# How a fused attention and MLP kernel makes the product of state and W1, and which engine rounds

## The chip, the cores and the metric

The kernel runs on one core of a Trainium2 chip. The metric is the device time of one execution in microseconds (us). The five instruction queues are those of TensorE (PE, matrix products), VectorE (DVE), ScalarE (ACT), GpSimd (POOL) and SyncE (SP, which issues the DMAs). "PEld" is PE's load of a stationary operand.

## What is computed

```python
def _attn_ref(x, state):                       # B, H, S, Ns, D = 8, 8, 512, 32, 64
    scores = scale * x @ state.T
    a = softmax(scores)                        # over the 32 state rows
    xread = a @ state
    a2 = softmax(scale * state @ x.T)          # over the 512 rows of x
    sread = a2 @ x
    return concatenate([xread, sread], axis=2)

h = attn @ w_in                                # 512 -> 1024
solu = h * softmax(h)
y = (layer_norm(solu) * g_ln) @ w_out          # 1024 -> 512
z = y @ w3                                     # 512 -> 2048
out = (z * sigmoid(1.702 * z)) @ w4            # 2048 -> 512
```

There are 8 batches of 512 rows of x and 32 rows of state per head: 4608 token rows in all. The weights arrive as 64-bit floats and are brought to float32 on the chip.

## The kernel before

**Numbers.** Most products are made from split operands: a float32 tile is written as hi + lo, both in the rounded format fp32r, and `mm3` (lines 421 to 424) issues hi x hi, hi x lo and lo x hi into the same PSUM tile. `split` (line 454) makes the pair: first a cast to hi, then lo = w - hi. A few products take plain float32 operands (fp32) and are one matmul in the code; the trace shows two for each.

**The state's product with W1.** Since xread @ W1 is a @ (state @ W1), the kernel makes V = state @ W1 for each batch and then multiplies the 512 rows of a by V. V has four tiles of 128 x 512 per batch: two groups g of four heads, two halves f of W1's 1024 columns. For batches 0 and 1 `state_w1` (line 664) makes a tile with two fp32 matmuls whose stationary operand is 64 columns of the transposed state (`stT`) and whose outputs are the two halves of one PSUM tile's partitions; ACT rounds it out of PSUM to `vhi`, and DVE subtracts for `vlo`. From batch 2 on (`DIRECT = 2`) `state_w1_both` (line 679) makes V of two batches at once, while the even one of the pair is in its turn. The two batches' transposed states are put side by side and split (`sthi`, `stlo`), and every product is a `mm3` of 128 columns with the split W1 (`W1s`). Its PSUM tile holds half a tile of each batch, so four copies for each (g, f) bring the halves into float32 tiles `v`, which then pass through `split` to `hi_v` and `lo_v`. The odd batch is called turned: in its scores, reads and copies the two head pairs of a group change places.

**Which engine.** A step may name several engines with costs. The cast of `split` and that of the attention rows (`ahi`, line 609) may go to ACT or DVE, the subtraction to POOL or DVE.

**Order.** Nothing is issued in the order of the code. Each call of `do` records a step with its tiles; `Plan.plan` puts all steps in an order, by due times worked out backwards from keys that PE's steps carry, by planned costs per engine and by the free tiles of the SBUF slots (71 of kind "s") and of the eight PSUM banks; `emit` then issues each engine's list. Each engine works through its own list in that order and waits at an instruction whose inputs aren't there. In the attention stage PE's list for one batch b holds the transposes of x (until batch 2; later ones are made by DMA and DVE), the scores (`psc`, line 571), the transposes of exp (`e2t`, line 621), the reads of x (line 633), the V steps, and between them the first MLP's products of the batches before (`mlp1`, `z_T` at line 827, `mlp1_out`). Also in this stage W3's blocks are converted (lines 443 to 451), summed (line 880), split and written back to HBM, in groups `w3_00`, `w3_10`, `w3_01` (a fourth comes later). The second MLP follows and keeps PE full.

Of the kernel before, what the change touches and what calls it, by code (L numbers as in the profile page):

```python
# [8 lines left out]
F32 = mybir.dt.float32  # L9
# [16 lines left out]
KF = 11.222  # L26
LOOK = 27.436
KR = 1.553
DIRECT = 2
W1S = 20.477  # L30
ATT = -0.491
ZL = 7.738
M1B = -7.631
VST = 25.191
RK = 6
LEAD = 62.849
KEEP = 5
# [306 lines left out]
def attention_solu_gelu(ctx: ExitStack, tc: tile.TileContext, x, state, w1, w2, g_ln, w3, w4, out):  # L344
# [52 lines left out]
    def PE(c):  # L397
        return [("pe", c)]
# [55 lines left out]
    def split(w, name, due, shape=(512,), pair=None, low=(("pool", 1.23), ("dve", .6))):  # L454

        hi, lo = pair or [tl("s", [P, *shape], F32R, f"{h}_{name}") for h in ("hi", "lo")]
        do([("act", .52), ("dve", .335)], lambda e: copy(e, hi(), w()), [w], [hi])
        do(list(low), lambda e: e.tensor_tensor(lo(), w(), hi(), op=ALU.subtract), [w, hi], [lo], key=due)  # L458
        return hi, lo

# [43 lines left out]
    def attention(b):  # L504
# [5 lines left out]
            n_step[0] += 1  # L510
            return base + (n_step[0] - 1) * SLOT / steps[0]

        both = b >= DIRECT
        turned = both and b % 2
        xt = {}
        load_x(b, 0)
        if not turned:
            load_state(b)
        for j in range(1, NP):
            load_x(b, j)  # L520

# [43 lines left out]
        def scores(g):  # L565
            p = tl("m", [P, 512], F32, f"psc{b}_{g}")

            def go(e):
                for i in range(2):
                    jj = i ^ turned  # L570
                    e.matmul(p()[64 * i:64 * i + 64, :], stT[b]()[:, g, 64 * jj:64 * jj + 64], xt[2 * g + jj](),
                             start=True, stop=True)

            do(PE(.9), go, [stT[b], xt[2 * g], xt[2 * g + 1]], [p], key())
# [31 lines left out]
            do(DVE(.6), lambda e: e.transpose(out=at(), in_=s1()), [s1], [at])  # L606
            hi = tl("s", [P, S], F32R, f"ahi{b}_{g}")
            lo = tl("s", [P, S], F32R, f"alo{b}_{g}")
            do([("act", .52), ("dve", .335)], lambda e: copy(e, hi(), at()), [at], [hi])
            do([("pool", 1.23), ("dve", .6)], lambda e: e.tensor_tensor(lo(), at(), hi(), op=ALU.subtract),  # L610
               [at, hi], [lo])
            A[b, g] = (hi, lo)
# [13 lines left out]
        def read_s():  # L626
            p = tl("m", [P, 512], F32, f"psr{b}")

            def go(e):
                for g in range(G):  # L630
                    for c in range(C):
                        for hl in range(HG):
                            e.matmul(p()[NS * hl:NS * hl + NS, g * D:(g + 1) * D],
                                     e2k[g]()[:, c, NS * hl:NS * hl + NS],
                                     xn[b, 2 * g + (hl // 2 ^ turned)]()[:, c, hl % 2, :],
                                     start=(c == 0), stop=(c == C - 1))

            do(PE(1.55), go, [e2k[0], e2k[1]] + [xn[b, j] for j in range(NP)], [p], key())
            sr = tl("t", [P, G, 2, D], F32, f"sr{b}")
            for g in range(G):  # L640
                do(DVE(.26), lambda e, g=g: e.tensor_scalar(
                    sr()[:, g], p()[:, g * D:(g + 1) * D].unsqueeze(1).to_broadcast([P, 2, D]),
                    r2[g]()[:, 1:2], None, op0=ALU.mult), [p, r2[g]], [sr])
            p2 = tl("m", [P, 512], F32, f"psrT{b}")

            def go2(e):
                for g in range(G):
                    e.transpose(p2()[:, g * P:(g + 1) * P], sr()[:, g].rearrange("p a d -> p (a d)"), ident)

            do(PE(.22), go2, [sr], [p2], key())  # L650
            for q in range(2):
                for a in range(2):
                    def go3(e, q=q, a=a):
                        pv = p2()[:, 0:G * P].rearrange("p (j a n) -> p j a n", a=2, n=NS)
                        o = xs[q]()[64 * a:64 * a + 64, :, b * NS:(b + 1) * NS]
                        if turned:
                            for j in range(2):
                                copy(e, o[:, j], pv[64 * a:64 * a + 64, 2 * q + 1 - j, a, :])
                        else:
                            copy(e, o, pv[64 * a:64 * a + 64, 2 * q:2 * q + 2, a, :])  # L660
                    c = 1 + bool(turned)
                    do([("act", .11 * c), ("dve", .13 * c)], go3, [p2], [xs[q]])

        def state_w1(g, f):
            p = tl("m", [P, 512], F32, f"pv{b}_{g}_{f}")
# [10 lines left out]
            do(DVE(.6), lambda e: e.tensor_tensor(lo(), p(), hi(), op=ALU.subtract), [p, hi], [lo])  # L676
            V[b, g, f] = (hi, lo)

        def state_w1_both():


            hi = tl("s", [P, G, 4, 64], F32R, f"sthi{b}")
            lo = tl("s", [P, G, 4, 64], F32R, f"stlo{b}")
            for i in range(2):
                st = stT[b + i]

                def part(t, i=i):
                    return t()[:, :, 1:3, :] if i else t()[:, :, 0:4:3, :]

                def src(st=st):  # L690
                    return st().rearrange("p g (j n) -> p g j n", j=2)

                do([("act", .29), ("dve", .2)], lambda e, part=part, src=src: copy(e, part(hi), src()), [st], [hi])
                do([("pool", .68), ("dve", .33)], lambda e, part=part, src=src: e.tensor_tensor(
                    part(lo), src(), part(hi), op=ALU.subtract), [st, hi], [lo])
            for f in range(2):
                for g in range(G):
                    v = [tl("s", [P, 512], F32, f"v{b + i}_{g}_{f}") for i in range(2)]
                    for jj in range(2):
                        p = tl("m", [P, 512], F32, f"pv{b}_{g}_{f}_{jj}")  # L700

                        def go(e, p=p, g=g, f=f, jj=jj):
                            wh, wl = W1s[2 * g + jj, f]
                            at = [t()[:, g, 2 * jj:2 * jj + 2, :].rearrange("p i n -> p (i n)") for t in (hi, lo)]
                            mm3(p(), *at, wh(), wl(), True, True)

                        do(PE(.65), go, [hi, lo, *W1s[2 * g + jj, f]], [p], key())
                        for side in range(2):
                            t = v[side ^ jj]
                            r = slice(64 * side, 64 * side + 64)  # L710
                            do([("act", .48), ("dve", .6)], lambda e, t=t, p=p, r=r: copy(e, t()[r, :], p()[r, :]),
                               [p], [t])
                    for i in range(2):
                        V[b + i, g, f] = split(v[i], f"v{b + i}_{g}_{f}", None)

        x_T(0)
        x_T(1)
        if not turned:
            state_T(b)
        e0 = scores(0)  # L720
        x_T(2)
        x_T(3)
        e2_T(0, e0)
        e1 = scores(1)
        n_step[0] += 1
        if both and not turned:
            load_state(b + 1)
            state_T(b + 1)
        e2_T(1, e1)
        read_s()  # L730
        if both and not turned:
            n_step[0] -= 1
            steps[0] = VST
            state_w1_both()
        if not both:
            for f in range(2):
                for g in range(G):
                    state_w1(g, f)


    n_tiles = {b: C for b in range(B)}
# [473 lines left out]
            prepare_up(k, q, (160, 230, 310)[n])  # L1215
    attention(0)
    for b in range(B):
        if b + 1 == DIRECT:
            for f in range(2):
                for k in range(KD):  # L1220
                    W1s[k, f] = split(W1[k, f], f"w1s_{k}_{f}", b * SLOT + W1S + 2 * (k + KD * f))
# [88 lines left out]
```

## Time and profile before

| what | us |
|---|---|
| median of 3 runs (1126.53 to 1130.48) | 1126.65 |
| the profiled execution, time | 1126.07 |
| its span in the trace | 1124.3 |
| PE busy | 1080.0 |
| DVE busy | 825.2 |
| ACT busy | 637.8 |
| POOL busy | 258.7 |

The span is what the trace covers of one execution. "Busy" is the union of an engine's instructions; matmuls are pipelined and overlap, so the sum of their durations is more than the time in which they run. A group's line gives its busy time, the mean of one in ns, and behind the second bar the idle time of the engine just before these instructions and what released it.

### The profile page before, as it was taken

To read this page: it belongs to the slowest core of one execution; us is meant where nothing else is said; L and a number is where in the kernel's file an instruction comes from. 1 tells how busy PE (TensorE), PEld (TensorE's weight loads), DVE (VectorE), ACT (ScalarE), POOL (GpSimd) and SP (SyncE) were. 2 spreads that over 40 slices of the span, in tenths; PEclk is the share of its full clock that TensorE was granted. 3 is DMA by queue.
4 is the path that set the end of the run, shared out by engine and by line. 5 is a ranking of instruction groups with operands and counts; after the bars stand their busy time and mean duration, and the time that the engine had idled before them with its cause. 6 is when DMAs were issued, how large, how long until landed. Compare 5 with 4: busy or idle time off the path is not lost.

```text
span 1124.3 us, 21689 instructions
## 1 busy us (share of the span) xinstructions
PE 1080.0 (96%) x8055; PEld 976.9 (87%) x8055; DVE 825.2 (73%) x1398; ACT 637.8 (57%) x1171; POOL 258.7 (23%) x218
## 2 busy tenths in 40 slices
PE   6798999799899999999999999999999999999998
PEld 2466677577677889999999999999999999999998
DVE  6999878988989746628757755634388888788874
ACT  6686756866868546547666656545244444344341
POOL 3865443743746701301111000000000000000000
PEclk8899999999999999999999999999999999999999
DMA  8214234568673569998667657559944254344431
GB/s 242 67 39 113 78 70 135 165 126 177 187 162 87 158 153 365 334 374 276 230 233 242 237 204 257 179 209 398 383 145 125 64 170 150 101 144 151 134 93 57
DMA packets 233082, 202.78 MB, mean 180 GB/s; under 512 B 128784, under 2 KB 174864, under 8 KB 232976
## 3 DMA queue, kind: packets, MB, share of 16 engines
q1 hardware_dynamic: 232880, 201.26, 57.3%
q8 instruction: 63, 1.03, 0.4%
q14 instruction: 43, 0.35, 0.1%
q10 hardware_dynamic: 96, 0.13, 0.1%
HBM read 113.25 MB, written 82.84 MB: 174 GB/s over the span
## 4 chain that ended last, share of the span: by engine, by line
PE 75%; DVE 13%; issue 3%; SPq 3%; POOL 3%; DMA 2%; ACT 1%; DVEq 0%; POOLq 0%; ACTq 0%
PE psum L1098 9%; PE psum L1100 9%; PE psum L1099 9%; PE psum L1010 9%; PE psum L1011 9%; PE psum L1012 9%; PE psum L422 5%; PE psum L423 5%; PE psum L424 4%; DVE w_w L449 1%; DVE w_w L444 1%; SPq L529 1%; POOL lo_w3s L458 1%; DVE w_w L447 1%; DVE u L775 1%
## 5 line engine op out<-in xcount | busy, mean ns | idle before, releaser
L1098 PE MATMUL psum<-w4r,hi_g 128*128 128x256 f32 x896 | 251.8, 281 | 1.6 <-DVE oc L1109 1.6
L1100 PE MATMUL psum<-w4r,lo_g 128*128 128x256 f32 x896 | 251.6, 281 | 0.0
L1099 PE MATMUL psum<-w4r,hi_g 128*128 128x256 f32 x896 | 251.6, 281 | 0.0
L1098 PEld LDWEIGHTS psum<-w4r,hi_g 128*128 128x128 f32 x896 | 169.1, 189 | 1.8 <-ACT hi_g L463 1.8
L1100 PEld LDWEIGHTS psum<-w4r,lo_g 128*128 128x128 f32 x896 | 169.3, 189 | 0.0
L1099 PEld LDWEIGHTS psum<-w4r,hi_g 128*128 128x128 f32 x896 | 169.0, 189 | 0.0
L463 ACT CAST hi_g<-a_g 128x512 fp32r<-128x512 f32 x124 | 75.4, 620 | 127.3 <-DVE a_g L880 87.1
L451 POOL TENSOR_TENSOR w_w<-w_w,raw_w 128x512 uint32<-128x512 uint32 x48 | 68.9, 1441 | 284.1 <-DVE w_w L449 206.1
L1022 DVE TENSOR_TENSOR c<-psum,u 128x512 f32<-128x512 f32 x64 | 44.1, 689 | 98.0 <-PE psum L1012 63.7
L422 PE MATMUL psum<-zhi,hi_w 128*128 128x512 f32 (+1 forms) x288 | 113.9, 395 | 1.3 <-DVE zlo L835 0.6
L424 PE MATMUL psum<-zhi,lo_w 128*128 128x512 f32 (+1 forms) x288 | 109.9, 382 | 0.0
L957 DVE TENSOR_TENSOR lo_g<-a_g,hi_g 128x512 fp32r<-128x512 f32 x128 | 84.0, 685 | 19.9 <-PE psum L1099 7.1
L994 ACT ACTIVATE t<-c 128x512 f32<-128x512 f32 x96 | 60.5, 632 | 50.0 <-DVE c L1022 49.9
L957 DVE TENSOR_TENSOR lo_g<-gr,hi_g 128x512 fp32r<-128x512 f32 x104 | 71.0, 685 | 11.8 <-ACT hi_g L463 9.2
L423 PE MATMUL psum<-zlo,hi_w 128*128 128x512 f32 (+1 forms) x208 | 78.3, 376 | 0.2
L463 ACT CAST hi_g<-gr 128x512 fp32r<-128x512 f32 x104 | 61.8, 618 | 28.4 <-PE psum L1099 14.4
L422 PEld LDWEIGHTS psum<-zhi,hi_w 128*128 128x128 f32 x288 | 54.2, 188 | 17.3 <-issue 4.1
L424 PEld LDWEIGHTS psum<-zhi,lo_w 128*128 128x128 f32 x288 | 54.1, 188 | 11.8 <-DVE lo_w L458 0.4
L1010 PE MATMUL psum<-hi_x,w3r_1h 128*128 128x256 f32 x224 | 63.1, 282 | 1.2 <-ACT u L1017 1.2
L1011 PE MATMUL psum<-lo_x,w3r_2h 128*128 128x256 f32 x224 | 63.1, 282 | 0.0
L1010 PE MATMUL psum<-hi_x,w3r_2h 128*128 128x256 f32 x224 | 63.0, 281 | 0.0
L1011 PE MATMUL psum<-lo_x,w3r_3h 128*128 128x256 f32 x224 | 63.0, 281 | 0.0
(261 smaller groups left out, 3101.9 us busy)
## 6 DMA issues: line engine op xcount, KB each, us to landing
g<-t SPq DMA_DIRECT2D x136, 256.0 KB, 3.4
gr<-g SPq DMA_DIRECT2D x136, 256.0 KB, 3.4
w4r<-w4k SPq DMA_DIRECT2D x56, 256.0 KB, 5.2
raw_w<-in_moe_w_in SPq DMA_DIRECT2D x24, 512.0 KB, 6.0
raw_w<-in_moe_w_out SPq DMA_DIRECT2D x24, 512.0 KB, 4.2
xb<-scr SPq DMA_DIRECT2D x34, 256.0 KB, 6.3
scr<-x SPq DMA_DIRECT2D x16, 512.0 KB, 3.6
out<-oc SPq DMA_DIRECT2D x32, 256.0 KB, 3.8
```

Source lines behind the costliest of these rows:

```text
L422: nc.tensor.matmul(o, lhi, rhi, start=first, stop=False)
L423: nc.tensor.matmul(o, lhi, rlo, start=False, stop=False)
L424: nc.tensor.matmul(o, llo, rhi, start=False, stop=last)
L451: do(POOL(1.23), lambda e: e.tensor_tensor(u(), u(), raw()[:, :, 0], op=ALU.add), [w, raw], [w], key=due)
L463: e.copy(o, i)
L957: do(DVE(.68), lambda e: e.tensor_tensor(flat_(lo), flat_(t), flat_(hi), op=ALU.subtract), [t, hi], [lo], key=due)
L1010: nc.tensor.matmul(o, wh()[:, k, cut], hi()[:, k, :], start=first and not mi + k, stop=False, **OPEN)
L1011: nc.tensor.matmul(o, wh()[:, k, cut], lo()[:, k, :], start=False, stop=False, **OPEN)
L1012: nc.tensor.matmul(o, wl()[:, k, cut], hi()[:, k, :], start=False, stop=bool(mi and k), **OPEN)
L1098: nc.tensor.matmul(o, hi()[:, mi, cut], wt[:, 0], start=first, stop=False, **OPEN)
L1099: nc.tensor.matmul(o, hi()[:, mi, cut], wt[:, 1], start=False, stop=False, **OPEN)
L1100: nc.tensor.matmul(o, lo()[:, mi, cut], wt[:, 0], start=False, stop=2 * j + mi == NM - 1 and u == 1, **OPEN)
```

## The change

Three things change. `state_w1_both`, `DIRECT`, `VST` and all that belongs to turned batches go: every batch loads and transposes its own state in its turn and makes its four tiles of V with `state_w1` from float32 W1. The split of W1 is still made, for the last product of the reads (`mlp1` of B), and now recorded one batch before the end (its due time moves from batch 1 to batch 6; the order that comes out still has it early), while the float32 tiles of W1 stay until the last batch's V. And the first step of `split` and the cast of the attention rows name ScalarE alone.

```diff
@@ split
-        do([("act", .52), ("dve", .335)], lambda e: copy(e, hi(), w()), [w], [hi])
+        do(ACT(.52), lambda e: copy(e, hi(), w()), [w], [hi])
@@ attention
-        both = b >= DIRECT
-        turned = both and b % 2
         xt = {}
         load_x(b, 0)
-        if not turned:
-            load_state(b)
+        load_state(b)
...
-            do([("act", .52), ("dve", .335)], lambda e: copy(e, hi(), at()), [at], [hi])
+            do(ACT(.52), lambda e: copy(e, hi(), at()), [at], [hi])
...
-                        if turned:
-                            for j in range(2):
-                                copy(e, o[:, j], pv[64 * a:64 * a + 64, 2 * q + 1 - j, a, :])
-                        else:
-                            copy(e, o, pv[64 * a:64 * a + 64, 2 * q:2 * q + 2, a, :])
-                    c = 1 + bool(turned)
-                    do([("act", .11 * c), ("dve", .13 * c)], go3, [p2], [xs[q]])
+                        copy(e, o, pv[64 * a:64 * a + 64, 2 * q:2 * q + 2, a, :])
+                    do([("act", .11), ("dve", .13)], go3, [p2], [xs[q]])
...
-        def state_w1_both():
...
-        if both and not turned:
-            load_state(b + 1)
-            state_T(b + 1)
         e2_T(1, e1)
         read_s()
-        if both and not turned:
-            n_step[0] -= 1
-            steps[0] = VST
-            state_w1_both()
-        if not both:
-            for f in range(2):
-                for g in range(G):
-                    state_w1(g, f)
+        for f in range(2):
+            for g in range(G):
+                state_w1(g, f)
@@ main loop
-        if b + 1 == DIRECT:
+        if b + 1 == B:
             for f in range(2):
                 for k in range(KD):
                     W1s[k, f] = split(W1[k, f], f"w1s_{k}_{f}", b * SLOT + W1S + 2 * (k + KD * f))
```

The order of PE is the same up to the scores of batch 2 and again in the second MLP. In between it moves. The line numbers of the changed kernel differ: its `mm3` stands at 420 to 422, its `state_w1` at 660, `vhi` and `vlo` at 664 and 665, the copies and casts of ACT at 461, and W3's sums at 823. Numbers behind a name are buffer numbers.

PE where V of batches 4 and 5 begins, before; `hi_w1s` and `sthi4` are the split W1 and the two split states, `zhi2_5` is work of batch 2's first MLP:

```order
L424 MATMUL psum_69<-hi_v3_1_1_1745,alo3_1_1775 128x512
L621 MATMUL psum_69<-ident_79,e2t4_1_2126 128x128 x4
L422 MATMUL psum_69<-hi_w1s_0_0_479,sthi4_1965 128x512
L423 MATMUL psum_69<-lo_w1s_0_0_536,sthi4_1965 128x512
L424 MATMUL psum_69<-hi_w1s_0_0_479,stlo4_1974 128x512
L422 MATMUL psum_69<-zhi2_5_2117,hi_w2_5_1178 128x512
L423 MATMUL psum_69<-zlo2_5_2131,hi_w2_5_1178 128x512
L424 MATMUL psum_69<-zhi2_5_2117,lo_w2_5_1188 128x512
L422 MATMUL psum_69<-hi_w1s_1_0_482,sthi4_1965 128x512
L423 MATMUL psum_69<-lo_w1s_1_0_604,sthi4_1965 128x512
L424 MATMUL psum_69<-hi_w1s_1_0_482,stlo4_1974 128x512
L422 MATMUL psum_69<-hi_w1s_2_0_554,sthi4_1965 128x512
```

PE at V of batch 4 in the changed kernel:

```order
L420 MATMUL psum_69<-zhi2_6_2109,hi_w2_6_1241 128x512
L421 MATMUL psum_69<-zlo2_6_2127,hi_w2_6_1241 128x512
L422 MATMUL psum_69<-zhi2_6_2109,lo_w2_6_1279 128x512
L660 MATMUL psum_69<-w_w1_2_0_380,stT4_1902 64x512
L660 MATMUL psum_69<-w_w1_3_0_384,stT4_1902 64x512
L660 MATMUL psum_69<-w_w1_0_1_401,stT4_1902 64x512
L660 MATMUL psum_69<-w_w1_1_1_414,stT4_1902 64x512
L420 MATMUL psum_69<-zhi2_7_2234,hi_w2_7_1283 128x512
L421 MATMUL psum_69<-zlo2_7_2249,hi_w2_7_1283 128x512
L422 MATMUL psum_69<-zhi2_7_2234,lo_w2_7_1294 128x512
L420 MATMUL psum_69<-zhi2_7_2234,hi_w2_7_1283 128x512
L421 MATMUL psum_69<-zlo2_7_2249,hi_w2_7_1283 128x512
```

The groups of three with the two states are gone; in their place two steps of V (four fp32 matmuls of 64 columns, for the tiles (1, 0) and (0, 1)) stand in one run between split matmuls.

ACT where the last V tiles of batch 4 are rounded, before; `v4_1_1` and `v5_1_1` are the float32 tiles, `w3s` the blocks of W3:

```order
L463 CAST hi_w3s5_00_2393<-a2_w3_00_2274 128x512
L781 ACTIVATE junk_84,sml3_3_2200<-u3_3_2355,sml3_3_2200 128x1024
L463 COPY xs1_521<-psum_69 64x2x32
L463 COPY xs0_517<-psum_69 64x2x32
L463 COPY v4_1_1_2375<-psum_69 64x512
L463 CAST hi_v4_1_1_2425<-v4_1_1_2375 128x512
L463 COPY v5_1_1_2380<-psum_69 64x512
L463 CAST hi_w3s6_00_2441<-a3_w3_00_2283 128x512
L463 COPY x2_2_0_2449<-psum_69 128x1024
L463 COPY x2_2_1_2466<-psum_69 128x1024
L833 ACTIVATE zhi3_0_2472<-psum_69,g_sb_81 128x512
L463 CAST hi_v5_0_0_2481<-v5_0_0_2222 128x512
```

ACT at the same V tile (`vhi4_1_1`) in the changed kernel:

```order
L664 CAST vhi4_1_0_2284<-psum_69 128x512
L441 ACTIVATE w_w3_0001_2289<-raw_w3_0001_2230 128x512
L443 ACTIVATE raw_w3_0001_2230<-raw_w3_0001_2230 128x512
L461 CAST hi_w3s0_00_2306<-w_w3_0000_2205 128x512
L461 CAST hi_w3s4_00_2309<-a1_w3_00_2271 128x512
L461 COPY x2_2_0_2319<-psum_69 128x1024
L776 ACTIVATE zhi3_0_2329<-psum_69,g_sb_81 128x512
L461 CAST hi_w3s5_00_2335<-a2_w3_00_2321 128x512
L461 CAST hi_w3s6_00_2344<-a3_w3_00_2327 128x512
L664 CAST vhi4_1_1_2355<-psum_69 128x512
L461 CAST hi_w3s1_00_2362<-w_w3_0001_2289 128x512
L776 ACTIVATE zhi3_1_2369<-psum_69,g_sb_81 128x512
```

The copies and the cast from SBUF became one cast from PSUM, and it now stands behind six operations on W3, a copy of batch 2's result and a piece of the first MLP.

DVE at the subtraction of the same tile, before:

```order
L775 SCALAR_TENSOR_TENSOR u3_3_2355,sml3_3_2200<-psum_69,u3_3_2355 128x1024
L835 SCALAR_TENSOR_TENSOR zlo2_7_2388<-psum_69,g_sb_81,zhi2_7_2365 128x512
L780 TENSOR_SCALAR sml3_3_2200<-sml3_3_2200 128x1
L880 TENSOR_TENSOR a4_w3_00_2396<-w_w3_0001_2202,a2_w3_00_2274 128x512
L465 CAST hi_w3s1_00_2402<-w_w3_0001_2202 128x512
L465 COPY xs0_517<-psum_69 64x2x32
L458 TENSOR_TENSOR lo_w3s1_00_2411<-w_w3_0001_2202,hi_w3s1_00_2402 128x512
L783 TENSOR_SCALAR sml3_3_2200<-sml3_3_2200 128x1
L465 COPY xs1_521<-psum_69 64x2x32
L465 CAST hi_w3s2_00_2428<-a4_w3_00_2396 128x512
L458 TENSOR_TENSOR lo_w3s2_00_2432<-a4_w3_00_2396,hi_w3s2_00_2428 128x512
L458 TENSOR_TENSOR lo_v4_1_1_2439<-v4_1_1_2375,hi_v4_1_1_2425 128x512
```

and in the changed kernel:

```order
L665 TENSOR_TENSOR vlo4_0_1_2287<-psum_69,vhi4_0_1_2278 128x512
L665 TENSOR_TENSOR vlo4_1_0_2295<-psum_69,vhi4_1_0_2284 128x512
L442 TENSOR_SCALAR w_w3_0001_2289<-w_w3_0001_2289 128x512
L445 TENSOR_SCALAR w_w3_0001_2289<-w_w3_0001_2289 128x512
L447 SCALAR_TENSOR_TENSOR w_w3_0001_2289<-raw_w3_0001_2230,w_w3_0001_2289 128x512
L823 TENSOR_TENSOR a2_w3_00_2321<-a1_w3_00_2271,w_w3_0000_2205 128x512
L823 TENSOR_TENSOR a3_w3_00_2327<-w_w3_0010_2083,w_w3_0000_2205 128x512
L456 TENSOR_TENSOR lo_w3s4_00_2337<-a1_w3_00_2271,hi_w3s4_00_2309 128x512
L778 SCALAR_TENSOR_TENSOR zlo3_0_2346<-psum_69,g_sb_81,zhi3_0_2329 128x512
L823 TENSOR_TENSOR a4_w3_00_2357<-w_w3_0001_2289,a2_w3_00_2321 128x512
L665 TENSOR_TENSOR vlo4_1_1_2364<-psum_69,vhi4_1_1_2355 128x512
```

The casts of W3's blocks are gone from DVE's list, four subtractions per batch read PSUM, and the last of the four stands behind W3's conversion and sums.

## Rows read from the trace of the kernel before

**Rows 1.** the page's part on busy time; columns: busy us, share of the span, instructions.

```profile
PE 1080.0 (96%) x8055; PEld 976.9 (87%) x8055; DVE 825.2 (73%) x1398; ACT 637.8 (57%) x1171; POOL 258.7 (23%) x218
```

**Rows 2.** windows of 28 us in the attention stage; busy us by engine, PE's clock, DMA.

```profile
196.00:224.00 28.00, 22.14 (x157) 16.16 (x156) 26.90 (x44) 23.12 (x42) 21.81 (x17) 1.00 0.53 158
...
252.00:280.00 28.00, 28.00 (x132) 22.00 (x131) 22.88 (x42) 17.39 (x38) 9.71 (x10) 1.00 0.81 172
...
sum 308.00, PE 287.13 PEld 214.41 DVE 269.58 ACT 219.60 POOL 165.03; mean PE 26.10 PEld 19.49 DVE 24.51 ACT 19.96 POOL 15.00
```

**Rows 3.** PE's groups by form: busy us, mean ns, idle us before them and releaser.

```profile
L422 PE MATMUL psum<-hi_v,ahi 128*128 128x512 f32 x96 | 39.5, 411 | 3.4 <-DVE xs L465 2.6 <-DVE u L775 0.9
...
L422 PE MATMUL psum<-hi_w1s,sthi 128*128 128x512 f32 x24 | 11.0, 457 | 5.8 <-DVE zlo L835 2.5 <-DVE sr L641 2.1 <-ACT v L463 0.6
```

**Rows 4.** timeline of PE, V of batches 4 and 5: start us, us, what.

```profile
200.54 0.40 PE L422 MATMUL psum<-hi_w1s,sthi 128*128 128x512 f32 x1
...
201.28 0.50 PE L422 MATMUL psum<-hi_w1s,sthi 128*128 128x512 f32 x1
...
202.07 0.40 PE L422 MATMUL psum<-zhi,hi_w 128*128 128x512 f32 x1
202.30 0.39 PE L423 MATMUL psum<-zlo,hi_w 128*128 128x512 f32 x1
...
203.46 0.39 PE L422 MATMUL psum<-hi_w1s,sthi 128*128 128x512 f32 x1
...
204.39 0.50 PE L422 MATMUL psum<-hi_w1s,sthi 128*128 128x512 f32 x1
...
208.87 0.65 PE L827 MATMUL psum<-ident,u 128*128 128x128 f32 x4
209.28 0.48 PE L422 MATMUL psum<-zhi,hi_w 128*128 128x512 f32 x1
```

**Rows 5.** timeline of PE: V steps of batch 1, then a score step of batch 5.

```profile
60.94 1.08 PE L671 MATMUL psum<-w_w,stT 128*64 128x512 f32 x4
61.95 0.44 PE L555 MATMUL psum<-ident,S 128*128 128x128 f32 x2
...
229.88 0.39 PE L424 MATMUL psum<-zhi,lo_w 128*128 128x512 f32 x1
230.20 1.08 PE L571 MATMUL psum<-xT,stT 128*64 128x512 f32 x4
231.21 0.50 PE L422 MATMUL psum<-zhi,hi_w 128*128 128x512 f32 x1
231.54 0.39 PE L423 MATMUL psum<-zlo,hi_w 128*128 128x512 f32 x1
```

**Rows 6.** groups of ACT, DVE and POOL by form that make V's parts.

```profile
L463 ACT COPY v<-psum 64x512 f32<-64x512 f32 x47 | 27.1, 580 | 5.2 <-PE psum L424 3.6 <-DVE v L465 0.9
...
L675 ACT CAST vhi<-psum 128x512 fp32r<-128x512 f32 x8 | 4.7, 587 | 3.7 <-PE psum L671 3.6
...
L458 DVE TENSOR_TENSOR lo_v<-v,hi_v 128x512 fp32r<-128x512 f32 x7 | 7.4, 1056 | 0.1
...
L676 DVE TENSOR_TENSOR vlo<-psum,vhi 128x512 fp32r<-128x512 f32 x8 | 5.4, 681 | 1.5 <-ACT vhi L675 1.5
...
L458 POOL TENSOR_TENSOR lo_v<-v,hi_v 128x512 fp32r<-128x512 f32 x17 | 24.7, 1456 | 9.4 <-ACT hi_v L463 7.2 <-DVE hi_v L465 2.2
```

**Rows 7.** DVE's groups by form that convert weights and form W3's sums.

```profile
L449 DVE SCALAR_TENSOR_TENSOR w_w<-raw_w,w_w 128x512 uint32<-128x512 uint32 x48 | 40.3, 850 | 0.8
...
L444 DVE TENSOR_SCALAR w_w<-w_w 128x512 f32<-128x512 f32 x48 | 31.8, 670 | 9.3 <-ACT w_w L443 8.9
...
L447 DVE TENSOR_SCALAR w_w<-w_w 128x512 uint32<-128x512 uint32 x48 | 25.9, 548 | 1.0
...
L880 DVE TENSOR_TENSOR a_w<-w_w,w_w 128x512 f32<-128x512 f32 x8 | 9.4, 1170 | 1.8 <-POOL w_w L451 1.8
...
L880 DVE TENSOR_TENSOR a_w<-a_w,w_w 128x512 f32<-128x512 f32 x4 | 3.8, 952 | 0.0
```

More of the change, by code (lines that the diff above doesn't have):

```diff
@@ L28 @@
 KR = 1.553
-DIRECT = 2
 W1S = 20.477
@@ L33 @@
 M1B = -7.631
-VST = 25.191
 RK = 6
@@ L569, in go @@
                 for i in range(2):
-                    jj = i ^ turned
-                    e.matmul(p()[64 * i:64 * i + 64, :], stT[b]()[:, g, 64 * jj:64 * jj + 64], xt[2 * g + jj](),
+                    e.matmul(p()[64 * i:64 * i + 64, :], stT[b]()[:, g, 64 * i:64 * i + 64], xt[2 * g + i](),
                              start=True, stop=True)
@@ L634, in go @@
                                      e2k[g]()[:, c, NS * hl:NS * hl + NS],
-                                     xn[b, 2 * g + (hl // 2 ^ turned)]()[:, c, hl % 2, :],
+                                     xn[b, 2 * g + hl // 2]()[:, c, hl % 2, :],
                                      start=(c == 0), stop=(c == C - 1))
@@ L677, in state_w1 @@
             V[b, g, f] = (hi, lo)
-        def state_w1_both():
[L682 to L695, printed above, removed]
-            for f in range(2):
-                for g in range(G):
[L698 to L714, printed above, removed]
         x_T(0)
         x_T(1)
-        if not turned:
-            state_T(b)
+        state_T(b)
         e0 = scores(0)
@@ L725, in attention @@
         n_step[0] += 1
-        if both and not turned:
-            load_state(b + 1)
-            state_T(b + 1)
         e2_T(1, e1)
         read_s()
-        if both and not turned:
-            n_step[0] -= 1
-            steps[0] = VST
-            state_w1_both()
-        if not both:
-            for f in range(2):
-                for g in range(G):
-                    state_w1(g, f)
+        for f in range(2):
+            for g in range(G):
+                state_w1(g, f)
     n_tiles = {b: C for b in range(B)}
```

## The prediction

> **What bounds the kernel now.** I read the page first: TensorE (PE) is busy 1080.0 of 1124.3 us [rows 1], so the time is the matmul work plus some 44 us in which PE waits. Then the windows, to see which stage the change touches: from 56 to 364 us (the attention stage of the eight batches, where V is made and used) PE is busy 287.13 of 308 us and so idle 20.9; VectorE (DVE) is busy 269.58 there, ScalarE (ACT) 219.60, GpSimd (POOL) 165.03 [rows 2]. The idle time is uneven: between 196 and 224 us, where V of batches 4 and 5 is made, PE is busy only 22.14 of 28 while DVE is at 26.90; between 252 and 280 PE has no idle time at all, with DVE at 22.88 [rows 2]. So PE is the bound, and the loss is where DVE is full. Last, PE's groups by form: what stood in front of the matmuls of the shared V product was 5.8 us of waiting, and in front of those that read its result 3.4 us [rows 3]. These 9.2 us are what the change can touch directly.
>
> **A PE duration is not its price.** A split matmul of 512 columns is drawn as 0.39 us, but the next one starts 0.23 us later (202.07 to 202.30) [rows 4]: they overlap. I price everything on PE by start to start.
>
> **What is removed on PE.** Per pair of batches (2/3, 4/5, 6/7) there are eight groups of three split matmuls, 72 matmuls in all, of which the 24 first ones have a row [rows 3]. A group that began at 200.54 let its successor start at 201.28 (0.74 us), the next ones took 0.79 (201.28 to 202.07) and 0.93 (203.46 to 204.39) [rows 4]. Mean 0.82, times 24 groups: 19.7 us.
>
> **What is added on PE.** Six batches get four steps each in plain float32, 24 steps; one such step of batch 1 takes 1.01 us from start to start (60.94 to 61.95) [rows 5]. That is 24.2 us. A step of this shape also loosens its surroundings: the matmul before a score step of the same shape takes 0.32 us (229.88 to 230.20) and the one behind it 0.33 (231.21 to 231.54) where 0.23 is usual [rows 5], so 0.2 us for each place at which such steps are put between split matmuls. In the new order the 24 steps stand at 16 places: 3.2 us. Sum 27.4, less 19.7: **PE gets 7.7 us more work**. Bounds: 24.2 - 19.7 = 4.5 with no edges, 29.0 - 19.7 = 9.3 with an edge for every step. I take 7.7, since the places are counted. PE is 93% busy in this stage, so nothing hides it except the 20.9 us of waiting.
>
> [...]
>
> **What is removed and added on the other engines.** ACT loses 47 half copies of V out of PSUM, 27.1 us, and gets 24 casts at 0.587 us, 14.1 us; DVE gets 24 subtractions straight from PSUM at 0.681 us, 16.3 us; seven subtractions of DVE (1.056 us each, 7.4 us) and 17 of POOL (24.7 us) go [rows 6]. The small casts and subtractions of the state tiles go too, and the copies of turned batches become half as many; both are small and I put them at nothing either way. The second part moves 12 casts (five of attention rows, seven of W3 and W4 blocks) from DVE to ACT: by the nearest row, a cast of this size at 0.587 us [rows 6], some 7 us on ACT and at most that much off DVE. So ACT is lighter by about 13.0 - 7.0 = 6 us, POOL by 25, and DVE, the full one, is about even: 16.3 in, 7.4 and the moved casts out.
>
> **What becomes of the waits.** In front of the product and of its readers 9.2 us were lost [rows 3]. The instructions go, but half of these waits had DVE work behind them (a reduction, a subtraction, the copies of read rows) that the next instruction will wait for as well: I take 4.6 us as gained, bounds 0 and 9.2. The work is also spread over both batches of a pair, where it stood in one.
>
> Against this stand new waits, because V is now made one batch ahead at most and not two. In the old order V of an odd batch was ready a batch early. In the new order the reader follows its product after few matmuls; at the shortest, ACT's cast and DVE's subtraction (0.587 + 0.681 = 1.27 us [rows 6]) fit, if nothing is queued ahead of them. Something is: on ACT the last cast of batch 4 (vhi4_1_1) stands behind the casts hi_w3s5 and hi_w3s6, which are now ACT's alone and wait for sums that DVE makes. Worked out for this place: from the end of the run of four V matmul instructions PE has 21 split matmuls (21 x 0.23 = 4.8), one V step (1.01) and 18 transposes (four of them start 0.41 us before the next instruction, 208.87 to 209.28 [rows 4], so 1.8) before it reads vhi4_1_1: 7.6 us. DVE in this time does vlo4_0_1 and vlo4_1_0 (behind a cast: 0.587 + 2 x 0.681 = 1.95), three operations on w_w3_0001 (0.670 + 0.548 + 0.850) and the sums a2 (0.952) and a3 (1.170) [rows 6, 7], which makes 6.1; then lo_w3s4, zlo3_0 and a4 (each at least as long as a vlo: 2.0) and vlo4_1_1 itself (0.68): 8.8 us. PE waits 1 us there by this, 2 or more if GpSimd slows DVE. There are three such W3 stages (batches 4, 6, 7). I put 1 us at each: 3 us, bounds 0 and 6.
>
> **The sum.** 7.7 more work, 4.6 less waiting, 3.0 new waiting: +6.1 us. Against the profiled execution's 1126.07 us (span 1124.3 and 1.8 around it) that is 1132.2. The median of the runs is 0.6 above the profiled one, within what runs differ by. 0.5%, about what a measurement of this kernel can tell from no change, is 5.6 us: the forecast lies on that edge.
>
> Edits at nothing: the state loads of odd batches (four DMA issues each on SyncE's queue) move behind weight loads, with several us before the state's transposes; W1's eight tiles stay in the slot pool until batch 7, where they went after batch 1, while the tiles of a second batch's V go. If the pool were short, loads would start late and PE would wait for a DMA; in the rows of before it is DVE and ACT that PE waits for [rows 3]. After 400 us the order of PE is the same, and PE has no room there.
>
> **Rivals.**
> *VectorE sets the pace and nothing moves.* For: DVE at 26.90 of 28 where PE waits most, and 88% over the stage [rows 2]; then PE's 7.7 us fall into its 20.9 us of waiting. Against: stretches such as 252 to 280, where PE is full [rows 2]. Time: 1126, between 1124 and 1129.
>
> *The release of GpSimd makes DVE faster.* A subtraction of two SBUF tiles takes DVE 1.056 us in this stage, one with its first operand in PSUM 0.681 [rows 6]; if POOL's work is what stretches it, each us of POOL removed gives (1.056 - 0.681) / 1.056 = 0.36 us back: 24.7 x 0.36 = 8.9 us of DVE, in the stage whose waits are DVE's. With the 4.6 us: 7.7 - 13.5 = -5.8, time 1120.3. [...] Against: POOL still has 165 - 25 = 140 us here [rows 2, 6], and lighter POOL draws other work from the planner.
>
> *V behind ACT's queue.* The waits for V cost 2 us at each W3 stage (6 us) and the old waits come back in other places, so that nothing is gained: 7.7 + 6 = 13.7, time 1139.8. It decides from the point at which DVE's queue ahead of a vlo is longer than the 7.6 us of PE work.
>
> **How the numbers follow.** Forecast 1132.2, chance 0.46; nothing moves 0.22; V behind ACT's queue 0.18; GpSimd's release 0.14. Half of the forecast's cases lie over the 0.5% edge, with the third rival some 0.43 slower; half of the forecast and most of the first rival are 0.44 within; 0.13 faster. The range takes in the bounds of the edges (4.5 and 9.3) and of the waits, and reaches into both outer rivals: 1121 to 1140.
>
> **What would show it.** Right: the new V steps 1.0 us from start to start, PE busy up by 6 to 9 us, PE's idle time between 56 and 364 us down by 1 to 3 at most or unchanged, waits in front of vhi readers in the three W3 stages. Wrong: idle time in this stage down by more than 8 us (GpSimd's release or smoothing), or V steps that cost less than 0.9 us because their neighbours overlap; or waits for DMA landings, which I put at nothing.

## The result and the profile after

The changed kernel takes 1134.38 us (median, 1133.14 to 1135.89), the kernel before on the same chip 1125.68: ratio 1.0073, 95% interval 1.0051 to 1.0094, some 8 us slower (the interval runs from 5.7 to 10.6). The forecast was 1132.2, in a range from 1121 to 1140. The profiled execution has a span of 1133.2 us, 8.9 more than before.

The page's part on busy time, answering to [rows 1]; then the windows of [rows 2], with the same columns (the clock is the first number behind POOL's):

```profile
PE 1090.8 (96%) x8079; PEld 972.1 (86%) x8079; DVE 816.7 (72%) x1393; ACT 617.6 (54%) x1124; POOL 230.0 (20%) x198
```

```profile
196.00:224.00 28.00, 21.70 (x155) 14.26 (x154) 26.40 (x40) 17.98 (x33) 20.67 (x17) 0.90 0.60 185
...
252.00:280.00 28.00, 28.00 (x129) 19.26 (x128) 20.05 (x39) 16.86 (x31) 6.98 (x7) 1.00 0.65 150
...
sum 308.00, PE 289.22 PEld 203.68 DVE 255.80 ACT 192.88 POOL 137.43; mean PE 26.29 PEld 18.52 DVE 23.25 ACT 17.53 POOL 12.49
```

PE is busy 10.8 us longer, and its idle time (span less busy) goes from 44.3 to 42.4 us. Added work, and waits that are down by little: so far this is the forecast's shape. One number was not foreseen. In the windows of before PE's clock stood at 1.00 [rows 2]; in the first window here it is 0.90. The timeline of PE in that stretch (start us, us, what, and in brackets the idle time before it with what ended it):

```profile
207.22 1.94 PE L660 MATMUL psum<-w_w,stT 128*64 128x512 f32 x8 [0.37 <-DVE u L718]
209.09 0.51 PE L420 MATMUL psum<-zhi,hi_w 128*128 128x512 f32 x1
...
213.94 1.08 PE L660 MATMUL psum<-w_w,stT 128*64 128x512 f32 x4
214.95 1.09 PE L770 MATMUL psum<-ident,u 128*128 128x128 f32 x8
219.60 0.69 PE L550 MATMUL psum<-ident,S 128*128 128x128 f32 x2 [3.56 <-DVE zlo L778]
221.49 1.12 PE L770 MATMUL psum<-ident,u 128*128 128x128 f32 x4 [1.20 <-DVE vlo L665]
222.26 0.78 PE L420 MATMUL psum<-vhi,ahi 128*128 128x512 f32 x1
222.83 0.63 PE L421 MATMUL psum<-vlo,ahi 128*128 128x512 f32 x1
223.26 0.63 PE L422 MATMUL psum<-vhi,alo 128*128 128x512 f32 x1
```

Behind the two waits the split matmuls start 0.43 us apart (222.83 to 223.26) where [rows 4] has 0.23. The windows of 4 us around it show a granted clock of 0.50 from 220 to 224 us; a granted 0.50 is called the lower clock from here on, 1.00 full clock.

```profile
216.00:220.00 4.00, 0.45 (x3) 0.29 (x2) 4.00 (x4) 1.93 (x4) 3.32 (x3) 0.80 0.37 143
220.00:224.00 4.00, 2.80 (x10) 2.23 (x9) 2.68 (x4) 2.97 (x5) 2.43 (x3) 0.50 1.02 380
224.00:228.00 4.00, 4.00 (x17) 2.92 (x17) 2.18 (x3) 1.54 (x3) 0.42 (x1) 0.85 0.99 281
```

It happens at three places: here, behind a wait of 1.89 us at 107.92, and behind this one, where three V steps take 5.31 us from start to start (305.19 to 310.50, granted 0.50):

```profile
299.03 1.08 PE L660 MATMUL psum<-w_w,stT 128*64 128x512 f32 x4
303.77 0.69 PE L642 MATMUL psum<-ident,sr 128*128 128x128 f32 x2 [3.66 <-DVE sr L635]
305.19 5.39 PE L660 MATMUL psum<-w_w,stT 128*64 128x512 f32 x12 [0.73 <-ACT xs L461]
310.50 0.50 PE L420 MATMUL psum<-zhi,hi_w 128*128 128x512 f32 x1
```

Behind the first two places fourteen split matmuls at the lower clock cost 2.8 us more than at full clock (0.23 each, 0.32 for the one right behind transposes), and these V steps 2.6 more than twelve such matmuls at full clock (2.73 us, shown below): 5.4 us lost in all. In the profiled execution of before no matmul behind 56 us ran at the lower clock (granted 1.00 from 56 to 1123 us). Both are single executions, and that of before is a good one: its mean granted clock is 0.992, while 59 executions of this kernel on record average 0.9895; the six of the changed kernel average 0.9858, the profiled one 0.985. Scaled by these means (0.0037 apart, where the two profiled ones are 0.0070), the clock's share in a usual execution is some 2.9 us, an estimate.

What PE waited for at 219.60 stands on DVE's timeline, in the first of the W3 stages; behind it GpSimd's in the same time:

```profile
210.32 1.28 DVE L665 TENSOR_TENSOR vlo<-psum,vhi 128x512 fp32r<-128x512 f32 x2
211.51 0.42 DVE L442 TENSOR_SCALAR w_w<-w_w 128x512 f32<-128x512 f32 x1
211.97 1.24 DVE L445 TENSOR_SCALAR w_w<-w_w 128x512 uint32<-128x512 uint32 x1
213.25 1.66 DVE L447 SCALAR_TENSOR_TENSOR w_w<-raw_w,w_w 128x512 uint32<-128x512 uint32 x1
214.82 0.68 DVE L823 TENSOR_TENSOR a_w<-a_w,w_w 128x512 f32<-128x512 f32 x1
215.43 1.78 DVE L823 TENSOR_TENSOR a_w<-w_w,w_w 128x512 f32<-128x512 f32 x1
217.13 1.75 DVE L456 TENSOR_TENSOR lo_w3s<-a_w,hi_w3s 128x512 fp32r<-128x512 f32 x1
218.81 0.74 DVE L778 SCALAR_TENSOR_TENSOR zlo<-psum,g_sb,zhi 128x512 fp32r<-128x512 f32 x1
219.47 1.37 DVE L823 TENSOR_TENSOR a_w<-w_w,a_w 128x512 f32<-128x512 f32 x1
220.75 0.68 DVE L665 TENSOR_TENSOR vlo<-psum,vhi 128x512 fp32r<-128x512 f32 x1
```

```profile
214.98 1.67 POOL L449 TENSOR_TENSOR w_w<-w_w,raw_w 128x512 uint32<-128x512 uint32 x1 [0.63 <-DVE w_w L447]
216.61 1.72 POOL L456 TENSOR_TENSOR lo_w3s<-a_w,hi_w3s 128x512 fp32r<-128x512 f32 x1
219.01 1.27 POOL L456 TENSOR_TENSOR lo_w3s<-a_w,hi_w3s 128x512 fp32r<-128x512 f32 x1 [0.68 <-ACT vhi L664]
```

This is the queue the forecast named (a2, a3, lo_w3s4, zlo3_0, a4, vlo4_1_1). But PE doesn't stand in front of the reader of V (222.26): it stands a few transposes ahead of it, in front of instructions that need PSUM banks which `zlo` and then `vlo` still read. The second of the two waits ends with `vlo4_1_1` itself (221.43), which the reader needs as well.

### The profile page after: what moved, and what is told of

It reads as the page before. It is cut to its first block, busy times and chain, and to the rows that moved or that the text cites. A ratio compares the mean times of both kernels' runs of the same rounds, so it can differ in the third digit from the quotient of the medians.

```text
span 1133.2 us, 21655 instructions
## 1 busy us (share of the span) xinstructions
PE 1090.8 (96%) x8079; PEld 972.1 (86%) x8079; DVE 816.7 (72%) x1393; ACT 617.6 (54%) x1124; POOL 230.0 (20%) x198
## 4 chain that ended last, share of the span: by engine, by line
PE 78%; DVE 10%; DMA 4%; SPq 3%; ACT 2%; issue 2%; POOL 1%; POOLq 0%; DVEq 0%; ACTq 0%
PE psum L1041 9%; PE psum L1042 9%; PE psum L1043 9%; PE psum L953 9%; PE psum L954 9%; PE psum L955 9%; PE psum L420 5%; PE psum L421 5%; PE psum L422 5%; SPq L749 2%; PE psum L660 2%; PE psum L770 1%; DVE w_w L442 1%; DVE w_w L447 1%; DMA raw_w<-in_moe_w_in 1%
## 5 line engine op out<-in xcount | busy, mean ns | idle before, releaser
L900 DVE TENSOR_TENSOR lo_g<-a_g,hi_g 128x512 fp32r<-128x512 f32 x128 | 84.1, 686 | 20.6 <-PE psum L1043 7.4
L953 PE MATMUL psum<-hi_x,w3r_0h 128*128 128x256 f32 x224 | 63.0, 281 | 0.2 <-DVE c L965 0.2
```

The costliest lines, as they stand in the source:

```text
L900: do(DVE(.68), lambda e: e.tensor_tensor(flat_(lo), flat_(t), flat_(hi), op=ALU.subtract), [t, hi], [lo], key=due)
L953: nc.tensor.matmul(o, wh()[:, k, cut], hi()[:, k, :], start=first and not mi + k, stop=False, **OPEN)
```

## The experiments

For each run: PE's busy time and its idle time (span less busy) in the profiled execution, and the ratio of its times to those of the kernel before on the same chip.

| run | PE busy | PE idle | ratio to before [95%] |
|---|---|---|---|
| before | 1080.0 | 44.3 | 1 |
| after | 1090.8 | 42.4 | 1.0073 [1.0051, 1.0094] |
| e1 casts only | 1083.3 | 46.8 | 1.0021 [1.0008, 1.0034] |
| e2 own V only | 1089.2 | 42.8 | 1.0053 [1.0035, 1.0072] |
| e3 after, short W3 | 1087.3 | 35.0 | 0.9973 [0.9961, 0.9984] |
| e4 before, short W3 | 1079.6 | 40.0 | 0.9933 [0.9913, 0.9953] |
| e5 V twice | 1106.6 | 35.9 | 1.0159 [1.0142, 1.0177] |
| e6 after, filled | 1094.0 | 41.2 | 1.0082 [1.0069, 1.0096] |
| e7 after, spread | 1088.1 | 37.1 | 0.9988 [0.9977, 0.9999] |
| e8 before, spread | 1081.0 | 42.4 | 0.9962 [0.9948, 0.9976] |
| e9 casts, spread | 1082.1 | 43.5 | 0.9985 [0.9972, 0.9997] |
| e10 before, spread 12 | 1086.1 | 51.6 | 1.0075 [1.0052, 1.0099] |

**The two parts apart.** e1 is the kernel before with the casts given to ScalarE; e2 is the changed kernel with the casts free again.

```diff
-        do([("act", .52), ("dve", .335)], lambda e: copy(e, hi(), w()), [w], [hi])
+        do(ACT(.52), lambda e: copy(e, hi(), w()), [w], [hi])
...
-            do([("act", .52), ("dve", .335)], lambda e: copy(e, hi(), at()), [at], [hi])
+            do(ACT(.52), lambda e: copy(e, hi(), at()), [at], [hi])
```

> The second part of the change alone: the casts that begin a split of weights or attention rows are ScalarE's, V is made for two batches at once as before. Theory A (the loss is PE's extra V work, 7.7 us, and new waits where V meets the W3 work in VectorE's queue; the casts hardly matter): within 3 us of the kernel before, PE busy within 2 us of 1080. Theory B (ScalarE's queue carries a real share of the loss): 3 us slower or more.

> The first part alone: every batch computes its V from float32 W1, the casts may go to ScalarE or VectorE as before. Theory A: slower by 7 to 10 us, as the whole change. Theory B: slower by 5 us or less.

e1's time lies within its theory A, though PE is busy 3.3 us more and not within 2; e2's 6.0 us lie between its two expectations. The casts give 2.4 us and V 6.0, each uncertain by 1.5 to 2, together the whole: within that the parts add, and V carries about three quarters. In e1 a wait that takes 2.29 us in before (at 291.38, with the same releaser) is 4.22 us long, and the granted clock in the 3 us behind it is 0.54, where before has 1.00:

```profile
294.81 1.11 PE L621 MATMUL psum<-ident,e2t 128*128 128x128 f32 x4 [4.22 <-ACT e2t L583]
295.57 0.78 PE L422 MATMUL psum<-zhi,hi_w 128*128 128x512 f32 x1
296.14 0.63 PE L423 MATMUL psum<-z,hi_w 128*128 128x512 f32 x1
```

**W3's share.** In both kernels the VectorE operations that convert W3's blocks of the three early stages work on 16 of 512 columns, in the same order. W3's values are then not those of the kernel: this work is left out.

```diff
-        do(DVE(.335), lambda e: e.tensor_scalar(w(), w(), TINY, TOP, op0=ALU.max, op1=ALU.min), [w], [w])
+        nn = 16 if name[:3] == "w3_" and name[3:5] != "11" else 512
+
+        do(DVE(.335), lambda e: e.tensor_scalar(w()[:, 0:nn], w()[:, 0:nn], TINY, TOP, op0=ALU.max, op1=ALU.min), [w], [w])
...
```

> The changed kernel, with the same planned order, in which the three VectorE operations that convert a W3 block work on 16 of 512 columns for the first three W3 groups (36 operations, some 25 us of VectorE; W3's values are left unconverted in the other columns). Theory A: the waits of PE at V of batches 4 and 6 (4.8 and 4.4 us) mostly go, and with them the stretches at half clock: 10 to 14 us faster than the changed kernel, about 1121 to 1124 us. Theory B: the waits stay, as ScalarE's list is unchanged: less than 4 us faster.

> The kernel before with the same shortening of the three VectorE operations on the first three W3 groups (W3's values are left unconverted in the other columns). Theory A: its waits at the W3 stages are shorter, so it gains 4 to 7 us (about 1119 to 1122 us), less than the changed kernel does, and what is left between the two is PE's V work: 5 to 8 us less the waits. Rival (PE's V work costs nothing, all the loss is waits): the two shortened kernels are within 2 us.

Against their own full versions the changed kernel gains 1.00% (11 us, within the 10 to 14 of its theory A) and the kernel before 0.67% (7.6 us, a little over its 4 to 7). Between the two 0.40% stays, 4.5 us (3.9 between the medians), of the 0.73% (8.2 us) between them as they are, so the rival of e4, at most 2 us apart, falls. Some 4 us of the change's cost hang on W3's work on DVE by this, a difference of ratios that are each uncertain by 1 to 2.5 us. Idle time of PE says the same: cutting W3 takes 4.3 us from before and 7.4 from after, and in e3 the waits that took 3.56, 1.20 and 3.66 us above are 1.15, 1.18 and 1.55. What stays is the trade that the forecast made outside W3: 7.7 us more busy, 5.0 less idle.

**The price of a V step.** e5 issues every V product of batches 2 to 7 twice into the same bank.

```diff
-                for jj in range(2):
-                    e.matmul(p()[64 * jj:64 * jj + 64, :], stT[b]()[:, g, 64 * jj:64 * jj + 64],
-                             W1[2 * g + jj, f](), start=True, stop=True)
+                for _ in range(2 if b >= 2 else 1):
+                    for jj in range(2):
+                        e.matmul(p()[64 * jj:64 * jj + 64, :], stT[b]()[:, g, 64 * jj:64 * jj + 64],
+                                 W1[2 * g + jj, f](), start=True, stop=True)
```

> The changed kernel with the two matmuls per half of every V product of batches 2 to 7 issued twice into the same PSUM bank (the second pass overwrites the first with the same values): 24 more V steps and nothing else. Theory A (TensorE's own work sets the pace outside the W3 stages): each added step costs about the step's own 1.0 us less what falls into a wait, so +18 to +26 us over the changed kernel, 1152 to 1160 us. Rival (VectorE sets the pace, TensorE's added work falls into waits): under +8 us, below 1142 us.

The ratio is 0.0086 above the changed kernel's, some 10 us, between both expectations: both miss. A doubled step takes 1.87 us from start to start (219.51 to 221.38) where a single one takes 1.01, so 24 of them add 20.6. PE is busy 15.8 us more: the steps are real work. But 6.5 us of idle time go, and none of the fourteen slow split matmuls is left; the lower clock comes at one place of the three (granted 0.50 in the 3 us behind a wait of 2.79 us at 309.91), where the V steps take 7.83 us for six, some 2.5 more than at 1.01 and 0.86 each. At the place shown above PE now stands 1.56 and 1.46 us, and keeps its clock (granted 1.00 in the 3 us behind each wait; 0.48 us drawn for the split matmul behind the transposes, not 0.78):

```profile
219.51 1.94 PE L661 MATMUL psum<-w_w,stT 128*64 128x512 f32 x8
221.38 1.10 PE L771 MATMUL psum<-ident,u 128*128 128x128 f32 x8
224.03 0.44 PE L550 MATMUL psum<-ident,S 128*128 128x128 f32 x2 [1.56 <-DVE zlo L779]
225.93 0.66 PE L771 MATMUL psum<-ident,u 128*128 128x128 f32 x4 [1.46 <-DVE vlo L666]
226.34 0.48 PE L420 MATMUL psum<-vhi,ahi 128*128 128x512 f32 x1
```

**Idle time and the clock.** e6 puts matmuls whose result is overwritten in front of the three places, with nothing else moved.

```diff
+    def idle_fill(p, n, key):
+        wh = W2[0][0]
+
+        def go(e):
+            for _ in range(n):
+                e.matmul(p(), wh()[:, 0:P], wh(), start=True, stop=True)
+        do(PE(.01), go, [wh], [p], key)
...
+            if b in (2, 6):
+                idle_fill(p2, 6 if b == 2 else 12, base + (n_step[0] + 1) * SLOT / steps[0] + .01)
...
+        if (b, k) == (3, 1):
+            idle_fill(p, 12, key - .01)
```

> The changed kernel with 30 extra matmuls of 512 columns whose result is overwritten (6, 12 and 12 of them, 6.9 us at 0.23 us each), put directly in front of the three instructions at which TensorE waits before its clock falls in the changed kernel: the transposes of the S read of batches 2 and 6 (107.9 and 303.8 us) and the z transposes ahead of the state transposes of batch 5 (214.9 us). Every engine's order stays as it is. If the fall to half clock follows from TensorE's standing idle there, the idle time shortens to under 1.5 us at each place, the granted clock stays at 1.00 after them, and the kernel is 3 to 6 us faster than the changed one although it does 6.9 us more of matmuls: 1128 to 1131 us. If the fall has another cause (the V steps themselves, the power of the stretch), the clock still falls at the three places and the time is that of the changed kernel or up to 3 us longer: 1134 to 1138 us.

Only one of the three places became the test that it was meant to be. Ahead of 219 us the twelve matmuls ran while PE would have stood, the wait in front of the state's transposes shrank from 3.56 to 0.79 us, and the clock held (granted 1.00 from 216 to 224 us):

```profile
215.16 3.02 PE L507 MATMUL psum<-hi_w 128*128 128x512 f32 x12
218.02 1.03 PE L781 MATMUL psum<-ident,u 128*128 128x128 f32 x8
219.84 0.44 PE L558 MATMUL psum<-ident,S 128*128 128x128 f32 x2 [0.79 <-DVE zlo L791]
221.73 0.66 PE L781 MATMUL psum<-ident,u 128*128 128x128 f32 x4 [1.45 <-DVE vlo L676]
222.15 0.48 PE L420 MATMUL psum<-vhi,ahi 128*128 128x512 f32 x1
222.47 0.40 PE L421 MATMUL psum<-vlo,ahi 128*128 128x512 f32 x1
```

At the two others the fill itself waited (1.90 and 3.69 us, ended by the same DVE instructions), so no idle time was filled. There the clock fell as in the changed kernel (granted 0.56 and 0.50 in the 3 us behind the waits), and the fill paid for it:

```profile
302.36 5.49 PE L507 MATMUL psum<-hi_w 128*128 128x512 f32 x12 [3.69 <-DVE sr L643]
307.65 0.63 PE L653 MATMUL psum<-ident,sr 128*128 128x128 f32 x2
309.01 2.80 PE L671 MATMUL psum<-w_w,stT 128*64 128x512 f32 x12 [0.73 <-ACT xs L461]
311.74 0.50 PE L420 MATMUL psum<-zhi,hi_w 128*128 128x512 f32 x1
```

Twelve fill matmuls take 5.29 us, and the V steps behind them 2.73, the full clock's 1.01 and twice 0.86, where the changed kernel took 5.31. So the steps are not what lowers the clock; for the power of a stretch no run has a number. All this is one profiled execution, and the last section shows a place whose clock came out both ways. The time, within 1 to 3 us of the changed kernel's, says nothing by itself, since some 7.7 us of fill were paid for.

**W3 spread in the plan.** Nothing is left out; the four blocks of a W3 stage become due 8 units apart and the seven split sums 3 apart, in the changed kernel (e7), in the kernel before (e8), and in e1 (e9). e10 is e8 with 12 and 5.

```diff
-        blocks = [to_f32(rows(w3, k + 2 * j, q + 2 * i), f"w3_{k}{q}{i}{j}", due - 3, keep=KEEP)
+        blocks = [to_f32(rows(w3, k + 2 * j, q + 2 * i), f"w3_{k}{q}{i}{j}", due - 3 - 8 * (3 - j - 2 * i), keep=KEEP)
...
-            for h, t in zip("hl", split(t, f"w3s{i}_{k}{q}", due)):
+            for h, t in zip("hl", split(t, f"w3s{i}_{k}{q}", due + 3 * i)):
```

> The changed kernel with the three early stages of W3's conversion spread in the plan: the four blocks of a stage due 8 units apart instead of together, and the seven split sums 3 units apart. No work is added or left out. If the burst of VectorE work in these stages is what costs the last 4 to 5 us of the change (waits of 3 to 4 us in front of TensorE, then half clock), the time falls to 1126 to 1130 us. If not, it stays at 1132 to 1136 us.

> The kernel before with the same spread of W3's conversion. By the theory that these bursts cost the kernel before about 4 us of waits: 1121 to 1125 us, and the changed kernel with the same spread stays 3 to 5 us above it. If the bursts cost it nothing: 1125 to 1128 us.

> The kernel before with the casts alone given to ScalarE, and with W3's conversion spread in the plan as in the two spread kernels. If the casts' 2.4 us of the unspread kernel come from a wait inside a W3 stage (the 4.2 us wait at 294.8 us and the half clock after it), they go with the spread: 1121 to 1125 us, within 1.5 us of the spread kernel before. If ScalarE's later casts cost TensorE time in every batch, the kernel stays 2 to 3 us above the spread kernel before: 1125.5 to 1127 us.

> The kernel before with W3's conversion spread further: the blocks of a stage 12 units apart and the split sums 5. If the burst of VectorE work is what makes TensorE wait in these stages, and the spread of 8 and 3 units left some of it, another 1 to 2 us go: 1121 to 1123 us. If what is left of the waits has other causes, the time is that of the first spread, 1123 to 1125 us, or more where the longer stage meets the next one.

The first two came out as the theory of the bursts has it, but for the distance between them, just under the 3 to 5 us expected. The changed kernel falls to 1126.59 us, 0.85% less and about level with before; before falls to 1123.65. The difference between them is 0.26%, 2.9 us, and again it is more work (7.1 us busy) against less idle time (5.3).

e9 stays 2.6 us (0.23%) above e8, as large as e1's cost and as its second theory has it, though its waits between 56 and 376 us sum to 17.2 us against e8's 18.4. What its profiled execution has and that of e8 has not is the lower clock: 17 split matmuls behind 124.1 and 354.5 us (granted 0.50 and 0.74 in the next 3 us) at 0.43 us from start to start, 3.6 us lost. The mean granted clock of their ten executions each points the same way (0.984 to 0.991 against 0.989 to 0.993). So the casts' cost isn't bound to the W3 stage. That the clock carries it, and why the casts bring it about, is not shown: e1 has nearly the same wait at this place (1.37 us at 124.42, 1.38 at 124.10 in e9) and keeps its clock there (granted 1.00).

e10 fell outside both ranges: 1136.89 us, a ratio of 1.0075, so as slow as the changed kernel. Its expectation left room for more "where the longer stage meets the next one"; no run here tells whether that is the cause. Its waits sum to 26.2 us, and the clock is low behind three of them (granted 0.54, 0.50 and 0.53 in the 3 us behind waits of 2.26, 3.20 and 2.12 us); one of these, with GpSimd's normalization as the releaser:

```profile
267.81 0.48 PE L827 MATMUL psum<-ident,u 128*128 128x128 f32 x1 [3.20 <-POOL u L786]
267.94 0.77 PE L422 MATMUL psum<-zhi,hi_w 128*128 128x512 f32 x1
```

So spreading W3 is no gain by itself. Each plan lays the waits elsewhere, and e8 and e10, two plans that differ only in these due times, lie 13 us apart. What to read in e7 and e8 is that the changed kernel's loss moves with W3's place. Each V step as one split product of the batch's own 64 columns was not tried, and its price is not shown.

## Why the prediction was right, point by point

**More work on PE: +7.7 forecast, bounds 4.5 to 9.3.** Right in kind, somewhat large. The 24 new steps take 25.6 us from start to start: ten that stand alone take 1.01 each, four pairs 1.87 each, and the two runs of three 2.73 and, at the lower clock, 5.31. Without the clock's 2.6 that is 23.0 and not 24.2, since a step right behind another adds 0.86. Their edges are some 2.1 us and not 3.2; what left took 18.8 and not 19.7. That makes +6.3. By the page it is less: 10.8 us more busy, of which 5.4 went at the lower clock, leaves 5.4. Both lie inside the bounds; e3 against e4 and e7 against e8 give 7.7 and 7.1, slow matmuls included. PE's busy time itself rose by more than the 6 to 9 us given as the sign of being right, because of the clock. That the edges belong to the steps of 64 columns, and are paid once for each place, is the author's estimate and not shown: 0.32 us also lie between two split matmuls behind transposes of 128 columns (222.15 to 222.47 in e6, shown above), where the stationary operand has 128 columns throughout.

**Half of the old 9.2 us of waits gained: -4.6.** Right. With W3's work on DVE cut the idle time falls by 5.0 us between the two kernels, with W3 spread by 5.3. The old groups' waits are gone (the readers of `vhi` have 0.0 us of idle before them, where [rows 3] had 3.4), and part of what stood behind them came back in front of others.

```profile
L420 PE MATMUL psum<-vhi,ahi 128*128 128x512 f32 x128 | 53.2, 416 | 0.0
```

**New waits in the W3 stages: +3, 1 us at each of three.** The sum was right, the single waits not. Idle time that goes when W3's work is cut is 7.4 us after and 4.3 before: +3.1. But the named place lost 4.8 us (3.56 and 1.20) instead of 1, another stage 3.7 (in front of the transposes of the S read, not of a reader of V), and the third none of this kind. The step that failed is the size of DVE's queue. It was put at 8.8 us from the end of the two V steps in one run (209.09); until `vlo4_1_1` was done (221.43) it took 12.3. PE's own work from 209.09 to the reader at 222.26 is 8.4 us, some of it at the lower clock, near the 7.6 forecast; and 12.3 less 7.6 is 4.7, the wait that came. The banks only put it ahead of the reader, which could not have had `vlo4_1_1` sooner.

What the sum had too short are the three operations on `w_w3_0001` (3.3 us against 2.1), `lo_w3s4`, `zlo3_0` and `a4` (3.6 against 2.0) and smaller parts. Those of two SBUF operands that meet GpSimd's work take 1.4 to 1.8 us, and end right behind it: `a3` at 217.21, `lo_w3s4` at 218.88 and `a4` at 220.84, each 0.55 us behind the end of a GpSimd instruction (216.65, 218.33, 220.28). The forecast had this as "2 or more if GpSimd slows DVE" and did not put it into the sum.

**What was missing: the clock.** Nothing in the sum stood for it, since before shows 1.00 in the windows read [rows 2]. 5.4 us were lost to it. So 5.4 of work, 5.4 of clock and 1.9 less of idle make the 8.9 us of the span; the forecast's 7.7 and -1.6 make 6.1. The nearness is partly luck: the work was put 1.4 to 2.3 too high, and a term was absent that is 5.4 in these two executions and some 3 in usual ones.

**The rivals.** "VectorE sets the pace" falls: PE's work showed in the time, and doubling it showed again. It was half right in e5, where 6.5 us of waits took up part of it. "GpSimd's release" falls: POOL is busy 28.7 us less, and the three conversions of [rows 7] average 822, 667 and 595 ns against 850, 670 and 548: no gain. What it started from, DVE taking longer beside GpSimd's work, shows in the trace all the same: a sum of two SBUF tiles takes DVE 0.68 us at 214.82, begun ahead of GpSimd's instruction at 214.98, and the next one 1.78 at 215.43, begun beside it. With 11% of POOL's work gone, the two still met at this place. A run with these GpSimd subtractions moved elsewhere was not made. "V behind ACT's queue" named its condition rightly, a DVE queue longer than PE's 7.6 us, and the queue was longer; but its 2 us a stage came as 4.8, 3.7 and none, and the old waits did not come back in full.

## What to carry to other kernels

Price a matmul by starts, and one right behind its like by the second start (0.86 us here, not 1.01). Price a queue on DVE with the durations that its operations have at that place, beside GpSimd's work, and not with those of a free stretch: 12.3 us came where 8.8 were summed. Such a queue can stop TensorE ahead of the reader, at the next instruction that needs a PSUM bank (3.56 us at 219.60). An engine that sits at its limit in bursts (DVE while W3 is converted, 26.40 of 28 us) can make a change in the order cost or gain several us, so measure a change under two plans before its cost is put down to its arithmetic: here 8 us with one plan, 3 with the other. A wait on TensorE can cost more than its length, since the clock may be lower behind it: here 0.50 behind 3.66 us of waiting, and three V steps in 5.31 us for 2.73.

## What the runs showed of the hardware

The clock behind a wait. Over the twelve traces (62 to 400 us), each of the nine waits of 2.79 us or more was followed by matmuls at the lower clock (granted 0.50 to 0.54 in the next 3 us). Of the waits between 1.8 and 2.5 us eight were followed by it (granted 0.53 to 0.74) and fifteen not (1.00), in kernels of both kinds, and it came behind shorter ones too: two of 1.15 and 1.18 us and one of 1.55 in e3 (0.82, 0.55 and 0.86), one of 1.38 in e9 (0.50). The same place with the same work ahead of it shows both: a wait of 1.89 us at 107.92 in the changed kernel left a granted 0.71 in the next 3 us, and in e7 the same wait at 106.80 left 1.00:

```profile
106.80 0.44 PE L642 MATMUL psum<-ident,sr 128*128 128x128 f32 x2 [1.89 <-DVE sml L723]
107.00 0.48 PE L420 MATMUL psum<-zhi,hi_w 128*128 128x512 f32 x1
107.32 0.40 PE L421 MATMUL psum<-zlo,hi_w 128*128 128x512 f32 x1
```

So idle time is shown as what goes ahead of it, and filling it kept the clock at one place (granted 1.00 in e6 where the changed kernel had 0.50); what decides in the short waits is not shown.

The clock also goes with the spread of one kernel's times: over 59 executions of the kernel before, on three chips, those with a mean granted clock of 0.991 or more average 1126.7 us (21), those at 0.986 or less 1130.3 (6).
